# Layer 1 of a three-stage kernel: the next unit's square, tanh and cube ahead of this unit's cast and low part

## The chip, the cores and the metric

One core of one Trainium2 chip runs the whole program. The metric is the device time of one launch in microseconds (us), as the median of several runs. TensorE (PE) multiplies matrices into eight banks of PSUM; VectorE (DVE) and ScalarE (ACT) read those banks and do the elementwise work; the SyncE queue (SP) issues the DMA transfers. Each engine works through its own instructions in the order in which the program gives them.

## The reference, cut to what matters

```python
# 1. attention inside chunks of 64 tokens: q, k, v are (4, 8, 576, 64)
scores = scale * np.matmul(q_c, k_c.transpose(0, 1, 2, 4, 3))
scores = scores - np.max(scores, axis=-1, keepdims=True)
attn = np.exp(scores)
attn = attn / (np.sum(attn, axis=-1, keepdims=True) + 1e-09)
out = np.matmul(attn, v_c)
x = out ... reshaped to (2304, 512)
# 2. layer 1: w_in (512, 2048), w_out (2048, 512)
h = x @ w_in
x = (h - np.tanh(h)) @ w_out
# 3. layer 2: the same shapes, other weights
h = x @ w_in
sp = np.where(h > 20.0, h, np.log1p(np.exp(np.minimum(h, 20.0))))
out = (h * np.tanh(sp)) @ w_out
```

## The kernel before, in words

The 2304 tokens are 18 tiles of 128 (`i` = 0 to 17), gathered into five blocks of 512, 256, 512, 512 and 512 tokens; block 1 is the short one. The 2048 hidden features are 16 units of 128. One step `s` is one unit of one block of one layer, so there are 160 steps: layer 1 is steps 0 to 79 (block 0 is steps 0 to 15, the short block steps 16 to 31, block 4 steps 64 to 79), layer 2 is steps 80 to 159.

Every product is made of three matmuls on a split operand: a high part (the value rounded to the matmul's format) and a low part (what the rounding left). In step `s` PE runs `gemm1(s)` (12 matmuls into one "hidden" bank, 4 or 5 by turns in layer 1) and then `gemm2` of the unit two steps back (three back in the short block), 12 matmuls that add into banks 0 to 3. After a block's last `gemm2`, `evacuate` takes banks 0 to 3 out, with one cast on ACT and one subtraction on DVE for each bank.

Between the two products of layer 1 the value h - tanh(h) is made from six or seven instructions:

- `gap_act`: the square `z` (ACT L314) and the tanh `t` (ACT L315), both read from the hidden bank;
- `gap_mid`: the cube `g` = z * h (DVE L320) and h - t (DVE, helper line L69, tile `t`), both read from the hidden bank; the second is the bank's last reader;
- `gap_poly`: a mask `m` and a second square of `z` (ACT L325, L326), from SBUF;
- `gap_end`: the polynomial (DVE L307) and the choice between the two forms (DVE L308);
- `hi_part`: the cast to the high part `go` (ACT L334); `lo_part`: its low part (DVE L69, tile `go`).

`gap_end`, `hi_part` and `lo_part` of a unit stand one step later than the rest. In step `s` the order before is: `gemm1(s)`; for unit `s - 1` its `gap_end`, cast and low part; for unit `s` its square, tanh, cube, difference and polynomial; then `gemm2`.

While block 0 runs, the weights of layer 1 arrive as 64-bit words and are turned into high and low parts, one unit per step: `w_turned` (ACT L89), `w_low` (DVE L99), `w_float` (DVE L108), `w_hi` (ACT L117), `w_lo` (DVE L69, tile `w`). While block 4 of layer 1 runs, `convert2` does the same for layer 2 at one or two pieces per step.

The attention of block 0's four tiles is done ahead of step 0, in an order written out by hand (the lead, which `run(...)` lists). The attention of the other tiles is spread over the steps of the block before theirs, each tile starting three steps after the one ahead of it. The plan `inner` is run between the elementwise work and `gemm2`, the plan `tail` at the step's end. For a tile the steps are: `a_scores` (PE L180, into banks 6 and 7), `a_first` (the maximum L187 and its subtraction on DVE, the exp L192 on ACT), `a_norm` one step later (four DVE instructions L197 to L200), `a_turn` two steps later (four PE transposes L207), `a_turned` (ACT copy L212), and three steps later `a_values` (PE L224) and `a_parts` (a cast on ACT L236 and a low part on DVE). PE also runs `warm`, transposes of the identity whose result is not used.

All banks are one tensor, `banks`. The framework that orders the engines writes the waits from the program's order and from what each instruction touches.

Of the kernel before, what the change touches and what calls it, by code (L numbers as in the profile page):

```python
# [27 lines left out]
P = 128  # L28
# [4 lines left out]
NF = DFF // P  # L33
# [3 lines left out]
BLOCKS = [512, 256, 512, 512, 512]  # L37
TMAX = 512
# [3 lines left out]
def attn_moe_moe(ctx, tc, qkv, w1, w2, out):  # L42

    nc = tc.nc
# [3 lines left out]
    block_of = [max(b for b in range(NB) if first[b] <= i) for i in range(NI)]  # L48
# [10 lines left out]
    ident = const.tile([P, P], F32, name="ident")  # L59
# [3 lines left out]
    banks = psum.tile([P, 8, 512], F32, name="banks")  # L63
# [4 lines left out]
    def sub(o, a, b, eng=None):  # L68
        (eng or nc.vector).tensor_tensor(o, a, b, op=ALU.subtract)  # L69
# [26 lines left out]
    def w_low(layer, f):  # L96

        lo = w_words(layer, f, I32)[0]
        nc.vector.tensor_scalar(lo, lo, 29, None, op0=ALU.logical_shift_right)  # L99
# [14 lines left out]
    def w_hi(layer, f):  # L114
        del W[layer, f, "raw"]
        w = W[layer, f] = wp.tile([P, 2, 2 * DM], F32R, tag=f"w{f}", name=f"w{f}")
        nc.scalar.copy(w[:, 0], W[layer, f, "f"])  # L117

    def w_lo(layer, f):
        w = W[layer, f]  # L120
        sub(w[:, 1], W.pop((layer, f, "f")), w[:, 0].bitcast(F32))
# [23 lines left out]
    def cast2():  # L145
        while casts:
            w_hi(1, casts.pop(0))
# [13 lines left out]
    def pair(i, n):  # L161


        return banks[:, BK[i]:BK[i] + 2, n * 2 * P:(n + 1) * 2 * P]

    def room(i, tag, early):

        if i < first[1]:
            return ep.tile([P, TMAX], F32, tag=early[i // 2 % len(early)], name=tag)
        return pools["a"].tile([P, TMAX], F32, tag=tag, name=tag, bufs=1)  # L170
# [23 lines left out]
    def a_norm(i):  # L194
# [4 lines left out]
        nc.vector.reciprocal(rd, rd)  # L199
        nc.vector.tensor_tensor(e, e, rd[:].unsqueeze(3).to_broadcast([P, 2, NP, CH]), op=ALU.mult)  # L200

    def a_turn(i):

        e = E[i].rearrange("p j n k -> p (j n k)")
        ps = pair(i, 0)
        for n in range(NP):
            nc.tensor.transpose(ps[:, n // 2, n % 2 * P:(n % 2 + 1) * P], e[:, n * P:(n + 1) * P], ident)  # L207

    def a_turned(i):
        del E[i]  # L210
        ET[i] = room(i, "et", "t")[:].rearrange("p (n t) -> p n t", n=NP)
        nc.scalar.copy(ET[i].rearrange("p (m n) t -> p m n t", m=2),  # L212
                       pair(i, 0).rearrange("p m (n t) -> p m n t", n=2))

    def a_values(i):

# [28 lines left out]
    def hidden(s):  # L245
        l, b, f = steps[s]
        n = 4 + s % 2 if l == 0 else 4 + (s - HALF) % 4
        return banks[:, n, :BLOCKS[b]]

    def gemm1(s):  # L250
        l, b, f = steps[s]
        w, x, ps = W[l, f], XL[l, b], hidden(s)
        n = 0
        for k in range(KD):
            for a, c in ((0, 0), (0, 1), (1, 0)):
                nc.tensor.matmul(ps, w[:, a, k * P:(k + 1) * P], x[:, c, k, :BLOCKS[b]],  # L256
                                 start=n == 0, stop=n == 3 * KD - 1)
                n += 1
# [42 lines left out]
    def valid(s, l):  # L301
        return 0 <= s < NS and steps[s][0] == l


    def gap_end(s):
        z, t, m, g = ZT.pop(s)
        nc.vector.scalar_tensor_tensor(g, z, PK, g, op0=ALU.add, op1=ALU.mult)  # L307
        nc.vector.copy_predicated(g, m.bitcast(I16), t)  # L308
        GF[s] = g

    def gap_act(s):
        ph = hidden(s)
        z, t, m, g = ZT[s] = temp(s, "z"), temp(s, "t"), temp(s, "m", BF16), temp(s, "g")
        nc.scalar.activation(z, ph, AF.Square)  # L314
        nc.scalar.activation(t, ph, AF.Tanh)  # L315

    def gap_mid(s):
        ph = hidden(s)
        z, t, m, g = ZT[s]
        nc.vector.tensor_tensor(g, z, ph, op=ALU.mult)  # L320
        sub(t, ph, t)

    def gap_poly(s):
        z, t, m, g = ZT[s]
        nc.scalar.activation(m, z, AF.Relu, bias=-C2)  # L325
        nc.scalar.activation(z, z, AF.Square, scale=SQ_SCALE, bias=SQ_BIAS)  # L326

    def hi_part(s):
        if lag(s) > LAG and s % 2:

            o = GO[s] = op.tile([P, 2, TMAX], F32R, tag="o", name="go")
        else:
            o = GO[s] = gp.tile([P, 2, TMAX], F32R, tag="go", name="go")
        nc.scalar.copy(o[:, 0, :BLOCKS[steps[s][1]]], GF[s])  # L334

    def lo_part(s):
        t = BLOCKS[steps[s][1]]
        sub(GO[s][:, 1, :t], GF.pop(s), GO[s][:, 0, :t].bitcast(F32))

    def mish(s):  # L340
        g = GF[s] = temp(s, "g")
        nc.scalar.activation(g, hidden(s), AF.Mish)  # L342
# [10 lines left out]
    for f in range(NF - 2):  # L353
        w_load(0, f)

    def warm(n):

        for _ in range(n):
            nc.tensor.transpose(banks[:, 7, 2 * P:3 * P], ident, ident)

    def a_first(i):
        a_max(i)
# [2 lines left out]
    def a_turns(i):  # L365
        a_turn(i)
        a_turned(i)
# [5 lines left out]
    def run(*todo):  # L373
        for what, *args in todo:
            what(*args)


    warm(8)
    run((a_scores, 0), (a_scores, 1), (a_scores, 2), (a_first, 0), (a_first, 1), (a_norm, 0), (a_turns, 0),
        (a_first, 2), (a_norm, 1), (a_values, 0), (a_turns, 1), (a_scores, 3), (a_first, 3), (a_part, 0, 0),  # L380
        (a_norm, 2), (a_part, 0, 1), (a_values, 1), (a_turns, 2), (a_part, 1, 0), (w_turned, 0, 0),
        (a_norm, 3), (a_part, 1, 1), (w_low, 0, 0), (a_values, 2), (a_turns, 3), (a_part, 2, 0), (a_part, 2, 1),
        (w_float, 0, 0), (a_values, 3), (warm, 8), (w_hi, 0, 0), (a_part, 3, 0), (a_part, 3, 1), (w_lo, 0, 0),
        (w_turned, 0, 1), (w_low, 0, 1), (w_float, 0, 1),
        (a_load, lead), (a_load, lead + 1), (w_load, 0, NF - 2), (w_load, 0, NF - 1),
        (w_turned, 0, 2), (w_low, 0, 2))

# [2 lines left out]
    inner, tail = {}, {}  # L390

    def at(plan, s, *todo):
        plan.setdefault(s, []).extend(todo)

    for b in range(1, NB):
        for q in range(BLOCKS[b] // P):
            i = first[b] + q
            BK[i] = 6
            s = (b - 1) * NF + (2 if BLOCKS[b] > 2 * P else 5) + 3 * q
            at(inner, s, (a_scores, i))  # L400
            at(tail, s, (a_first, i))
            at(tail, s + 1, (a_norm, i))
            at(inner, s + 2, (a_turn, i))
            at(tail, s + 2, (a_turned, i))
            at(inner, s + 3, (a_values, i))
            at(tail, s + 3, (a_parts, i))
            if i + 2 < NI:
                at(tail, s + 3, (a_load, i + 2))

    LAG = 2  # L410
    done = 0
# [1 line left out]
    def lag(s):  # L413

        l, b, f = steps[s]
        return LAG + (l == 0 and BLOCKS[b] < TMAX)

    last = (NB - 1) * NF
    for s in range(NS + LAG):

        j = s - last
        if j == 0:
            es.close()
            pools["out"] = ctx.enter_context(tc.tile_pool(name="late", bufs=1))
        if s == HALF:
            nc.scalar.preload_act_table_set("mish")
        u = s + 2
        if s < NS:
            gemm1(s)
        if u - 1 < NF:  # L430
            w_hi(0, u - 1)
        if valid(s - 1, 0):
            gap_end(s - 1)
            hi_part(s - 1)
        if valid(s - 1, 1):
            hi_part(s - 1)
            lo_part(s - 1)
        if u - 1 < NF:
            w_lo(0, u - 1)
        if valid(s - 1, 0):  # L440
            lo_part(s - 1)
        if valid(s, 0):
            gap_act(s)
            gap_mid(s)
            gap_poly(s)
        if valid(s, 1):
            mish(s)
        cast2()
        run(*inner.get(s, []))
        if u < NF:  # L450
            w_float(0, u)
        while done < min(NS, s + 1) and done + lag(done) <= s:
            gemm2(done)
            done += 1
        if u + 1 < NF:
            w_turned(0, u + 1)
            w_low(0, u + 1)
        run(*tail.get(s, []))

        f = j - LAG - 1  # L460
        if 0 <= f < NF:
            w_load(1, f)
        f = j - LAG - 3
        if 0 <= f < NF:
            (w_turned if f < TURNED else w_rebias)(1, f)
        if LAG + 5 <= j < NF:
            convert2(1 if j % 3 else 2, j - LAG - 4)
        elif j >= NF and j != NF + 1:
            convert2(2, j - LAG - 4)
        if s < NS:  # L470
            l, b, f = steps[s]
            if f == 5 and l == 0 and b == NB - 1:
                x_load(0)
            if f == 5 and l == 1 and b + 1 < NB:
                x_load(b + 1)
# [37 lines left out]
```

## Time and profile before

| | |
|---|---|
| median of 3 runs | 890.13 us (890.1 to 890.99) |
| the profiled execution's own time | 888.45 us |
| its span, first to last instruction | 886.7 us |
| busy: PE, DVE, ACT | 843.2, 480.8, 400.6 us |
| mean granted clock of TensorE | 0.988 |

The profiled execution took 1.75 us more than its span, and 1.68 us less than the median of the runs. Busy times are sums over instructions; a busy PE is not PE at its peak, since the ends of matmuls are modelled.

### The profile page before, as it was taken

Reading aid. Unit: us, or ns where it says so; the run is one execution under the profiler, and the core shown is the slowest. Engines: PE = TensorE matmul, PEld = TensorE weight load, DVE = VectorE, ACT = ScalarE, POOL = GpSimd, SP = SyncE. Lnnn points to the kernel's source line nnn. Section 1 sums busy time; section 2 is a strip of 40 time slices with the busy share of each in tenths; the row PEclk is TensorE's granted clock in tenths of the full one; section 3 lists DMA queues with packets and bytes.
Section 4 is the critical chain, followed back from the end, with each engine's and each line's share of the span. In section 5 each row is a group of like instructions: output and inputs, shape, how many; then the busy total and the mean of one; then the engine's idle time right before and its main releaser. Section 6 shows DMA issues by size and latency. Waiting matters only on the chain.

```text
span 886.7 us, 12059 instructions
## 1 busy us (share of the span) xinstructions
PE 843.2 (95%) x4984; PEld 700.0 (79%) x4984; DVE 480.8 (54%) x736; ACT 400.6 (45%) x704; POOL 6.4 (1%) x11
## 2 busy tenths in 40 slices
PE   5798898989999999999998999999999999999998
PEld 4586777887888878888886788898888888888886
DVE  5799997776777677767788984111111111111111
ACT  3677775555555555455776543232222222222221
POOL 0000000000000000000001000000000000000000
PEclk9799999999999999999999999999999999999999
DMA  9940102221111131006754510030300030001001
GB/s 375 420 178 6 60 7 96 72 70 51 37 37 36 59 109 36 1 1 214 295 199 147 183 55 1 1 143 1 119 0 1 1 143 0 1 1 48 0 1 48
DMA packets 16903, 72.08 MB, mean 81 GB/s; under 512 B 1488, under 2 KB 3536, under 8 KB 12240
## 3 DMA queue, kind: packets, MB, share of 16 engines
q1 hardware_dynamic: 16848, 71.31, 21.7%
q8 instruction: 39, 0.64, 0.3%
q14 instruction: 16, 0.13, 0.1%
HBM read 57.15 MB, written 14.16 MB: 80 GB/s over the span
## 4 chain that ended last, share of the span: by engine, by line
PE 69%; DVE 21%; ACT 6%; issue 1%; ACTq 0%
PE banks L256 33%; PE banks L270 22%; PE banks L267 12%; DVE g L320 3%; DVE wf L108 3%; DVE g L308 3%; DVE g L307 2%; DVE w L69 2%; DVE t L69 2%; ACT go L334 2%; ACT z L314 2%; ACT t L315 2%; DVE w L99 1%; DVE x L69 1%; DVE go L69 1%; ACT z L326 1%
## 5 line engine op out<-in xcount | busy, mean ns | idle before, releaser
L256 PE MATMUL banks<-x,w 128*128 128x512 f32 (+1 forms) x1920 | 426.2, 371 | 7.6 <-ACT w L117 3.1
L256 PEld LDWEIGHTS banks<-x,w 128*128 128x128 f32 x1920 | 340.0, 190 | 73.2 <-DVE w L69 5.2
L69 DVE TENSOR_TENSOR go<-g,go 128x512 fp32r<-128x512 f32 (+1 forms) x160 | 102.4, 640 | 321.2 <-ACT go L334 321.1
L267 PE MATMUL banks<-go,w 128*128 128x512 f32 (+1 forms) x960 | 217.4, 375 | 6.1 <-ACT go L334 3.5
L270 PE MATMUL banks<-w,go 128*128 128x512 f32 x864 | 209.0, 389 | 0.0
L334 ACT CAST go<-g 128x512 fp32r<-128x512 f32 (+1 forms) x160 | 92.5, 578 | 252.3 <-PE banks L270 136.3
L267 PEld LDWEIGHTS banks<-go,w 128*128 128x128 f32 x960 | 167.7, 190 | 39.2 <-ACT go L334 4.8
L270 PEld LDWEIGHTS banks<-w,go 128*128 128x128 f32 x864 | 161.2, 188 | 32.8 <-DVE x L69 0.2
L342 ACT ACTIVATE g<-banks 128x512 f32<-128x512 f32 (+1 forms) x80 | 44.5, 556 | 140.0 <-PE banks L256 139.2
L320 DVE TENSOR_TENSOR g<-z,banks 128x512 f32<-128x512 f32 (+1 forms) x80 | 50.7, 634 | 28.8 <-ACT t L315 26.7
L326 ACT ACTIVATE z<-z 128x512 f32<-128x512 f32 (+1 forms) x80 | 47.2, 590 | 23.9 <-DVE g L320 23.9
L308 DVE COPY_PREDICATED g<-m,t 128x512 f32<-128x512 int16 (+1 forms) x80 | 54.7, 684 | 2.8
L307 DVE SCALAR_TENSOR_TENSOR g<-z,g 128x512 f32<-128x512 f32 (+1 forms) x80 | 50.6, 633 | 5.2 <-ACT z L326 5.2
L69 DVE TENSOR_TENSOR t<-banks,t 128x512 f32<-128x512 f32 (+1 forms) x80 | 50.4, 630 | 0.0
L314 ACT ACTIVATE z<-banks 128x512 f32<-128x512 f32 (+1 forms) x80 | 44.1, 551 | 10.3 <-PE banks L256 10.2
L325 ACT ACTIVATE m<-z 128x512 bf16<-128x512 f32 (+1 forms) x80 | 47.0, 588 | 0.0
L315 ACT ACTIVATE t<-banks 128x512 f32<-128x512 f32 (+1 forms) x80 | 43.8, 548 | 0.0
L69 DVE TENSOR_TENSOR w<-wf,w 128x1024 fp32r<-128x1024 f32 x32 | 39.1, 1223 | 2.8 <-ACT w L117 2.8
L117 ACT CAST w<-wf 128x1024 fp32r<-128x1024 f32 x32 | 33.5, 1046 | 5.0 <-DVE wf L108 5.0
L207 PE MATMUL banks<-ident,e 128*128 128x128 f32 x72 | 13.2, 313 | 19.2 <-DVE e L200 19.2
L69 DVE TENSOR_TENSOR x<-banks,x 128x512 fp32r<-128x512 f32 (+1 forms) x38 | 23.8, 659 | 14.1 <-ACT x L236 10.7
L192 ACT ACTIVATE e<-e 128x512 f32<-128x512 f32 x18 | 11.4, 632 | 36.1 <-DVE e L69 36.1
(33 smaller groups left out, 274.0 us busy)
## 6 DMA issues: line engine op xcount, KB each, us to landing
w<-w SPq DMA_DIRECT2D x32, 1024.0 KB, 10.4
qkv<-qkv SPq DMA_DIRECT2D x18, 768.0 KB, 4.5
x<-x SPq DMA_DIRECT2D x16, 512.0 KB, 4.3
x<-x SPq DMA_DIRECT2D x4, 2048.0 KB, 8.5
out<-out SPq DMA_DIRECT2D x18, 256.0 KB, 2.1
x<-x SPq DMA_DIRECT2D x4, 256.0 KB, 2.7
x<-x SPq DMA_DIRECT2D x1, 1024.0 KB, 8.5
```

Of the source, the lines that this page charges most:

```text
L69: (eng or nc.vector).tensor_tensor(o, a, b, op=ALU.subtract)
L256: nc.tensor.matmul(ps, w[:, a, k * P:(k + 1) * P], x[:, c, k, :BLOCKS[b]], start=n == 0, stop=n == 3 * KD - 1)
L267: nc.tensor.matmul(banks[:, m, :t], w[:, a, DM + m * P:DM + (m + 1) * P], g[:, c, :t], start=start, stop=stop)
L270: nc.tensor.matmul(banks[:, m], g[:, a, m * P:(m + 1) * P], w[:, c, DM:], start=start, stop=stop)
L307: nc.vector.scalar_tensor_tensor(g, z, PK, g, op0=ALU.add, op1=ALU.mult)
L308: nc.vector.copy_predicated(g, m.bitcast(I16), t)
L314: nc.scalar.activation(z, ph, AF.Square)
L315: nc.scalar.activation(t, ph, AF.Tanh)
L320: nc.vector.tensor_tensor(g, z, ph, op=ALU.mult)
L325: nc.scalar.activation(m, z, AF.Relu, bias=-C2)
L326: nc.scalar.activation(z, z, AF.Square, scale=SQ_SCALE, bias=SQ_BIAS)
L334: nc.scalar.copy(o[:, 0, :BLOCKS[steps[s][1]]], GF[s])
```

## The change

In layer 1 the step's order becomes: `gemm1(s)`; `gap_end(s - 1)`; `w_lo` of the next weights; square, tanh, cube and difference of unit `s`; the cast of unit `s - 1`; mask and second square of unit `s`; the low part of unit `s - 1`. For the four tiles of block 2 (6 to 9), whose attention runs under the short block, scores, maximum, exp and norm come one step earlier, transposes and values stay in the step where they were, and the transposes are written to the second half of banks 4 and 5 (`turn_room`) where the short block's `gemm1` fills only the first half. The lead is written in another order, with more `warm` transposes, and those in bank 5 in place of 7, save for the last eight.

```diff
+    def short(i):
+        return block_of[i] > 0 and BLOCKS[block_of[i] - 1] < TMAX
...
+    def turn_room(i):
+        if short(i):
+
+            return banks[:, 4:6, 2 * P:4 * P]
+        return pair(i, 0)
+
     def a_turn(i):
-        ps = pair(i, 0)
+        ps = turn_room(i)
...
         nc.scalar.copy(ET[i].rearrange("p (m n) t -> p m n t", m=2),
-                       pair(i, 0).rearrange("p m (n t) -> p m n t", n=2))
+                       turn_room(i).rearrange("p m (n t) -> p m n t", n=2))
...
-    def warm(n):
+    def warm(n, bank=7):
         for _ in range(n):
-            nc.tensor.transpose(banks[:, 7, 2 * P:3 * P], ident, ident)
+            nc.tensor.transpose(banks[:, bank, 2 * P:3 * P], ident, ident)
...
-    warm(8)
-    run((a_scores, 0), (a_scores, 1), (a_scores, 2), (a_first, 0), (a_first, 1), (a_norm, 0), (a_turns, 0),
-        (a_first, 2), (a_norm, 1), (a_values, 0), (a_turns, 1), (a_scores, 3), (a_first, 3), (a_part, 0, 0),
-        (a_norm, 2), (a_part, 0, 1), (a_values, 1), (a_turns, 2), (a_part, 1, 0), (w_turned, 0, 0),
-        (a_norm, 3), (a_part, 1, 1), (w_low, 0, 0), (a_values, 2), (a_turns, 3), (a_part, 2, 0), (a_part, 2, 1),
-        (w_float, 0, 0), (a_values, 3), (warm, 8), (w_hi, 0, 0), (a_part, 3, 0), (a_part, 3, 1), (w_lo, 0, 0),
-        (w_turned, 0, 1), (w_low, 0, 1), (w_float, 0, 1),
+    run((warm, 14, 5), (a_scores, 0), (warm, 2, 5), (a_scores, 1), (warm, 2, 5), (a_scores, 2), (warm, 4, 5),
+        (a_first, 0), (a_first, 1), (a_norm, 0), (a_turn, 0), (a_scores, 3), (a_turned, 0), (a_first, 2),
+        (a_norm, 1), (a_values, 0), (a_turn, 1), (w_turned, 0, 0), (a_max, 3), (a_part, 0, 0), (a_turned, 1),
+        (a_exp, 3), (a_norm, 2), (a_values, 1), (a_turn, 2), (a_part, 0, 1), (a_part, 1, 0), (a_turned, 2),
+        (a_norm, 3), (a_values, 2), (a_turn, 3), (a_part, 1, 1), (w_low, 0, 0), (w_float, 0, 0), (a_part, 2, 0),
+        (a_turned, 3), (a_part, 2, 1), (a_values, 3), (warm, 8), (w_hi, 0, 0), (w_low, 0, 1), (a_part, 3, 0),
+        (w_lo, 0, 0), (a_part, 3, 1), (w_turned, 0, 1), (w_float, 0, 1),
         (a_load, lead), (a_load, lead + 1), (w_load, 0, NF - 2), (w_load, 0, NF - 1),
         (w_turned, 0, 2), (w_low, 0, 2))
...
-            s = (b - 1) * NF + (2 if BLOCKS[b] > 2 * P else 5) + 3 * q
+            s = (b - 1) * NF + (1 if short(i) else 2 if BLOCKS[b] > 2 * P else 5) + 3 * q
             at(inner, s, (a_scores, i))
             at(tail, s, (a_first, i))
             at(tail, s + 1, (a_norm, i))
-            at(inner, s + 2, (a_turn, i))
-            at(tail, s + 2, (a_turned, i))
-            at(inner, s + 3, (a_values, i))
-            at(tail, s + 3, (a_parts, i))
+
+            t = s + 2 + short(i)
+            at(inner, t, (a_turn, i))
+            at(tail, t, (a_turned, i))
+            at(inner, t + 1, (a_values, i))
+            at(tail, t + 1, (a_parts, i))
             if i + 2 < NI:
-                at(tail, s + 3, (a_load, i + 2))
+                at(tail, t + 1, (a_load, i + 2))
...
         if valid(s - 1, 0):
             gap_end(s - 1)
-            hi_part(s - 1)
...
         if u - 1 < NF:
             w_lo(0, u - 1)
-        if valid(s - 1, 0):
-            lo_part(s - 1)
         if valid(s, 0):
             gap_act(s)
             gap_mid(s)
+        if valid(s - 1, 0):
+            hi_part(s - 1)
+        if valid(s, 0):
             gap_poly(s)
+        if valid(s - 1, 0):
+            lo_part(s - 1)
```

## Rows read from the trace of the kernel before

**Rows 1.** The page's busy time of each engine, with its share of the span.

```profile
PE 843.2 (95%) x4984; PEld 700.0 (79%) x4984; DVE 480.8 (54%) x736; ACT 400.6 (45%) x704; POOL 6.4 (1%) x11
```

**Rows 2.** Windows: stretch, its length, busy us and instructions by engine, granted clock, DMA.

```profile
0.00:28.97 28.97, 16.37 (x288) 13.07 (x288) 16.43 (x31) 10.86 (x16) 0.70 (x6) 0.88 0.95 385
47.66:133.04 85.38, 78.14 (x449) 61.90 (x448) 82.76 (x114) 62.18 (x95) 0.00 (x0) 0.98 0.13 49
218.19:492.00 273.81, 269.51 (x1630) 219.25 (x1628) 204.92 (x310) 161.37 (x278) 3.40 (x3) 1.00 0.27 97
```

**Rows 3.** Waits of PE, 133 to 200 us: us in total, times, longest.

```profile
PE banks L207 <- DVE e L200: 9.6, 4, 4.0
```

**Rows 4.** Waits of PE, 470 to 495 us.

```profile
PE banks L267 <- ACT go L334: 3.5, 3, 1.4
```

**Rows 5.** Timeline of the lead and step 0: start, us, instruction, idle before it.

```profile
1.36 1.97 PE L359 MATMUL banks<-ident 128*128 128x128 f32 x8 [1.36 <-POOL ident masks.py:199]
...
16.75 0.69 DVE L187 TENSOR_REDUCE mx<-banks 128x8 f32<-128x512 f32 x1 [2.30 <-PE banks L180]
...
28.23 0.69 DVE L69 TENSOR_TENSOR x<-banks,x 128x512 fp32r<-128x512 f32 x1 [1.65 <-ACT x L236]
...
30.11 6.88 PE L256 MATMUL banks<-x,w 128*128 128x512 f32 x22 [0.40 <-DVE w L69]
...
35.38 0.69 DVE L320 TENSOR_TENSOR g<-z,banks 128x512 f32<-128x512 f32 x1 [1.05 <-ACT t L315]
```

**Rows 6.** Timeline of SP's queue: the weight loads issued first.

```profile
2.96 24.58 SPq L75 DMA_DIRECT2D w<-w  x14
```

**Rows 7.** DMA issues of 2.9 to 3.2 us: transfers, KB each, us to landing.

```profile
w<-w SPq DMA_DIRECT2D x1, 1024.0 KB, 11.8
```

**Rows 8.** A window of 2 us within step 0's first product.

```profile
32.00:34.00 2.00, 2.00 (x6) 1.54 (x5) 1.49 (x2) 1.04 (x1) 0.00 (x0) 0.50 1.02 426
```

**Rows 9.** Timeline of one step of block 0.

```profile
52.93 0.68 DVE L69 TENSOR_TENSOR go<-g,go 128x512 fp32r<-128x512 f32 x1
53.02 0.59 ACT L315 ACTIVATE t<-banks 128x512 f32<-128x512 f32 x1
...
53.64 0.69 DVE L320 TENSOR_TENSOR g<-z,banks 128x512 f32<-128x512 f32 x1
54.24 0.68 DVE L69 TENSOR_TENSOR t<-banks,t 128x512 f32<-128x512 f32 x1
```

**Rows 10.** The cube's line over the whole trace: idle before it, us and times.

```profile
  ACT t L315: 26.7, 51
```

**Rows 11.** Windows from one tile's transposes to the next's in the short block.

```profile
152.58:166.20 13.62, 12.06 (x140) 11.66 (x140) 9.61 (x23) 6.73 (x18) 0.00 (x0) 0.87 0.17 59
166.20:178.78 12.58, 10.56 (x140) 10.16 (x140) 9.63 (x23) 6.64 (x18) 0.00 (x0) 1.00 0.20 64
```

**Rows 12.** Timeline of the short block around one tile's transposes.

```profile
178.78 0.66 PE L207 MATMUL banks<-ident,e 128*128 128x128 f32 x4 [2.02 <-DVE e L200]
...
179.90 0.38 ACT L314 ACTIVATE z<-banks 128x256 f32<-128x256 f32 x1
...
180.03 0.42 DVE L69 TENSOR_TENSOR go<-g,go 128x256 fp32r<-128x256 f32 x1 [0.47 <-ACT go L334]
...
180.93 0.42 DVE L69 TENSOR_TENSOR t<-banks,t 128x256 f32<-128x256 f32 x1
...
182.75 0.65 PE L180 MATMUL banks<-qkv 64*64 64x64 f32 x32
```

**Rows 13.** Timeline: PE at the end of the short block's evacuation.

```profile
215.34 3.02 PE L267 MATMUL banks<-go,w 128*128 128x512 f32 x12 [1.98 <-DVE x L69]
```

**Rows 14.** Timeline of one step of block 4, layer 2's weights in conversion.

```profile
471.03 0.69 DVE L69 TENSOR_TENSOR go<-g,go 128x512 fp32r<-128x512 f32 x1 [0.74 <-ACT go L334]
...
472.01 0.69 DVE L320 TENSOR_TENSOR g<-z,banks 128x512 f32<-128x512 f32 x1 [0.29 <-ACT t L315]
```

**Rows 15.** Chain of waits that ended last, a full-clock stretch: start, us, what.

```profile
236.49 2.72 PE banks L256 x12
```

## Prediction

> **What bounds the kernel now.** I read the page's busy times first: PE is busy for 95% of the span, 843.2 us, so 43.5 us of idle PE is about all that an order of instructions can win, apart from slow clock [rows 1]. Then the windows by stage, which show where the idle time lies. In the lead (0 to 29 us) PE is busy 16.4 of 29.0 us; in block 0, DVE is busy 82.8 of 85.4 us and PE 78.1, so DVE sets the pace; from 218 to 492 us PE is busy 269.5 of 273.8 us, so the 512-token blocks of layer 1 are bound by PE but for 4.3 us [rows 2]. Next the waits of PE. In the short block, PE waits four times at a tile's transposes for that tile's norm, 9.6 us in all [rows 3]; late in block 4 it waits for the cast and the low part of the unit that `gemm2` needs, 3.5 us for the cast alone, which is most of the 4.3 [rows 2, 4]. Last the timelines of these places, for what each engine waits for in turn. The gain is thus to be sought in four places: lead, block 0, short block, end of block 4.
>
> **The lead.** DVE waits there three times that the new order touches: 2.30 us for the scores of tile 3, which stood behind tile 1's transposes, 1.65 us for the cast of tile 3 [rows 5], and about 1 us more between. With scores 3 right behind tile 0's transposes, DVE goes from tile 1's norm straight to tile 3's maximum, 2.4 us earlier. I followed the new list with the durations that the trace has for the same instructions: tile 3's low part, on which the first `gemm1` waits, ends near 25.2 to 26.0 us in place of 28.92 [rows 5]. A new wait: `w_turned` of unit 0 is moved up in ACT's queue to about 13.6 us, and its weights land at 2.96 + 11.8 = 14.8 us [rows 6, 7]. Behind it wait tile 0's cast, tile 1's copy and tile 3's exp; this costs ACT 1.2 us but tile 3's norm on DVE, their first consumer on the path, still finds the exp done, so I take 0.3 us at the end.
>
> The first `gemm1` then runs 12 matmuls. Of the 22 that began at 30.11, ten finished the first `gemm1` by about 34.2 us, for the square was free to start at 35.38 - 1.05 - 0.1 [rows 5]: about 0.41 us each, at a granted clock of 0.50 (1.2 GHz) [rows 8]. At full clock 12 take 2.72 us [rows 15]; at half clock 4.95. So it ends between 25.2 + 2.7 = 27.9 and 26.0 + 4.95 = 31.0, and the first cube comes 1.14 us later, at 29.1 to 32.1 in place of 35.38: a gain of 3.3 to 6.3 us. The new lead leaves PE shorter pauses, so I take 5.0, a little above the middle. The cost of the extra `warm` transposes is nothing while they fit into the wait for q and k; they do at 14 x 0.25 us from 1.36 us on [rows 5], and the later groups of two and four also end before the next arrival. If they didn't, each would cost at most 0.25 us.
>
> **Block 0.** Here DVE works without pause, so only what shortens its own sequence counts. The cube starts at 53.64, when ACT's tanh has ended (53.02 + 0.59), and 0.71 us after the low part started; independent instructions follow each other at 0.60 (53.64 to 54.24) [rows 9]. With square and tanh ahead of the cast, the tanh is done before DVE comes to the cube, which saves 0.11 us in some eleven steps, 1.2 us. One step gives 0.3 back, where PE, just past a wait for a norm, delivers its hidden bank late. Net 0.9. Cast and low part are later by about 1.2 us; `gemm2` needs them only a step later.
>
> **The short block.** The same reordering cuts DVE's wait for the cast (0.47 us a step here [rows 12]), but PE decides. The four waits for a norm go, since now a step lies between norm and transposes. What is late next is the place that the transposes write: banks 4 and 5, where ACT and DVE still read this step's hidden bank. Do instructions that touch different columns of a bank wait for each other? The cube needs only `z` and the bank, yet it starts when the tanh, a mere reader of the same bank, has ended; 26.7 us of idle time in 51 places end so [rows 10]. No row shows it for different columns, so the bounds are: no wait, or a wait until the bank's last reader, the difference, is done. I take the wait, being the nearest row. From the square's start to the difference's end are 180.93 + 0.42 - 179.90 = 1.45 us [rows 12]; with 0.05 to start, PE stands 1.5 us in place of 2.02 [rows 12]. A period of three steps is PE's 10.56 us of work plus that: 12.1 in place of 12.58 [rows 11]. DVE agrees: its 9.63 us of work [rows 11] plus a wait for the scores (0.8) and one for the next square and tanh (1.4) is 11.8. Three periods: gain 1.4.
>
> The Trainium skill's page "PSUM — Partial Sum Buffer", section "PSUM bank collisions raise a hardware error", says that two engines at one bank collide also at disjoint columns and that waits should guard the bank and not the address. By it the transposes wait and the sum is the one below; by the rows alone, which show one range of columns, the time of rival (a) stays open too. The trace agrees as far as the cube's waits go [rows 10]; no row shows other columns.
>
> Against this stand two losses at the block's start. Scores of tile 6 move ahead of the last `gemm2` of block 0, 0.6 us of PE [rows 12]. And DVE, on which the first transposes wait in either order, does one unit more between the evacuation and them: choice, polynomial, cube and difference, four instructions of 0.42, 1.7 us, against two waits of 0.47 for a cast that it no longer has [rows 12]: 0.7 later. The drop of the clock to 0.87 in the first period [rows 11] follows a 4.0 us wait [rows 3], and there is one as long now. 1.4 - 0.6 - 0.7 - 0.4 for the clock (the scores now run in it too) = -0.3.
>
> At the block's end the evacuation stands behind ACT's square of `z`; with square and tanh before the cast that comes 0.7 us earlier, and PE's wait of 1.98 us [rows 13] shrinks as much: +0.7.
>
> **Block 4.** With layer 2's weights in conversion DVE falls behind, by the low part's wait for its cast, 0.74, and the cube's for the tanh, 0.29, a step [rows 14]. Both go: the cube and the difference now lie between the choice and the low part while the cast runs. That is 1.03 us a step over nine steps against the 4.3 us that PE idles [rows 2], after which PE's 2 x 2.72 = 5.44 us a step [rows 15] binds again. I take 4.0.
>
> **Elsewhere** blocks 2 to 4 stay bound by PE: a cast now waits for its step's `gemm1` and the low part ends some 3 us behind it, while `gemm2` needs it 5.4 us behind it. The loads of q, k and v keep their step and are issued as before. Layer 2 is untouched.
>
> **Sum.** 5.0 + 0.9 - 0.3 + 0.7 + 4.0 = 10.3 us. The profiled execution's 888.45 becomes 878.15 (span 886.7 to 876.4); the median of the runs shown lies 1.68 us above it, so 879.8.
>
> **Rivals.** (a) Transposes in another half of a bank don't wait. Then the four waits of 9.6 us [rows 3] go, and the slow clock of the first period with them (1.0, 13.62 against 12.58 [rows 11]), less the 0.6 + 0.7 lost at the start: 9.3 in place of -0.3, 870.2. For it speaks that DVE's 9.63 is less than PE's 10.56; against it the cube's waits. 0.17. (b) The lead stays at half clock, and ACT's wait for the weights reaches the path: 3.0 in place of 5.0 there, and with the cold start of the short block worse by 2, a sum of 6.3: 883.8. For it speaks the clock of 0.50 at 32 us [rows 8], against it the shorter pauses. 0.15. (c) Slower: the later cast binds in the PE-bound steps. It decides once the low part ends more than 5.4 us behind `gemm1`; at 0.5 us beyond, in some 45 steps of blocks 2 to 4, it costs 22 us against 10.3: 891.6. Against it speak 2.4 us of slack and PE's 269.5 of 273.8 [rows 2]; a tile's maximum and norm take up to 2 us of DVE but stand behind the low part. 0.03. (d) Nothing moves, since what the lead wins is waited for later: the DMA or a wait that I don't see. 889 to 891. 0.03.
>
> **Numbers.** The forecast has 0.62, with its own range 876 to 883. The whole range must leave out 2 in 10: 868 to 885 takes in (a) and most of (b). Changes under 0.2% (1.8 us) can't be told from none. Faster: 0.62 + 0.17 + 0.15 = 0.94; same 0.03; slower 0.03.
>
> **What would show it.** The first square near 29 to 31 us; in block 0 cube pitches of 0.60 behind the weights' low part; at the short block's transposes waits of PE for the difference (tile `t`) in place of the norm; no wait for `go` at 470 to 495 us; DVE idle before a low part near none. Wrong would be: transposes that start right behind `gemm1`, a first `gemm1` past 27 us, or waits of `gemm2` for `go` in blocks 2 and 3.

## The result and the profile after

The changed kernel takes **879.23 us** (median of 4, 877.69 to 882.58) against 890.12 us before in the same measurement: ratio **0.9884 [0.9853, 0.9915]**, so 10.3 us faster by the ratio, at the least 7.6 (the medians lie 10.9 apart). Predicted were 879.8 us and 10.3 us.

The profiled execution of the changed kernel, 882.58 us with a span of 880.8, is the longest of its four; the same kernel measured again (`e1_after_again` below) took 878.77, and its profiled execution 879.07 with a span of 877.3. Both traces are used, since they differ where the clock does.

The page's busy times after:

```profile
PE 848.1 (96%) x4998; PEld 706.7 (80%) x4998; DVE 471.8 (54%) x736; ACT 400.1 (45%) x704; POOL 6.9 (1%) x11
```

Against [rows 1], PE has 14 instructions more (the added `warm` transposes) and 32.7 us idle in place of 43.5. DVE's busy time fell by 9 us with the same 736 instructions, whose durations add up to 502.8 us before and 503.7 after. So the page's busy time is not the sum over instructions that it was called above: two that follow each other without a wait start 0.60 us apart and last 0.69 [rows 9], the time in which they overlap counts once, and more of them now overlap.

Where the time went is read by cutting both spans at the same instructions: the first `gemm1`, the first `gemm1` of the short block (step 16) and of block 2 (step 32), that of step 35, which follows the evacuation's wait, and the first `gemm2` of layer 2. Windows of before (columns: stretch, length, busy us and instructions of PE, PEld, DVE, ACT, POOL, granted clock, DMA share, GB/s):

```profile
29.00:133.04 104.04, 93.19 (x496) 73.06 (x497) 99.69 (x135) 75.56 (x114) 0.00 (x0) 0.95 0.29 115
133.04:199.85 66.81, 57.02 (x645) 54.02 (x644) 50.23 (x112) 35.84 (x97) 0.00 (x0) 0.97 0.23 79
199.85:218.19 18.34, 16.36 (x118) 13.86 (x117) 13.53 (x25) 10.69 (x23) 0.00 (x0) 1.00 0.10 34
218.19:497.52 279.33, 274.90 (x1653) 223.58 (x1652) 209.41 (x315) 165.59 (x285) 3.40 (x3) 1.00 0.27 95
```

The same of the changed kernel, the profiled execution of the result:

```profile
24.79:129.16 104.37, 94.14 (x497) 74.69 (x497) 97.70 (x135) 75.67 (x114) 0.00 (x0) 0.93 0.33 131
129.16:200.98 71.82, 62.40 (x645) 58.36 (x644) 47.80 (x112) 36.17 (x96) 0.00 (x0) 0.90 0.22 74
200.98:218.70 17.72, 16.36 (x118) 13.85 (x117) 12.78 (x24) 10.14 (x22) 0.00 (x0) 1.00 0.10 34
218.70:491.59 272.89, 272.89 (x1654) 224.06 (x1652) 204.37 (x315) 164.37 (x284) 3.36 (x3) 1.00 0.27 97
```

And of the same kernel measured again, with its periods of three steps in the short block, from one tile's transposes to the next's, behind them:

```profile
25.32:127.80 102.48, 90.89 (x498) 71.27 (x497) 97.75 (x135) 76.09 (x115) 0.00 (x0) 0.98 0.33 132
127.80:197.62 69.82, 60.42 (x645) 56.43 (x644) 47.78 (x112) 36.22 (x96) 0.00 (x0) 0.93 0.22 77
197.62:215.34 17.72, 16.36 (x118) 13.86 (x117) 12.76 (x24) 10.14 (x22) 0.00 (x0) 1.00 0.10 34
215.34:488.20 272.86, 272.86 (x1654) 224.30 (x1653) 204.20 (x316) 165.35 (x286) 3.80 (x3) 1.00 0.27 97
...
147.56:162.59 15.03, 13.45 (x142) 12.56 (x143) 9.21 (x23) 6.87 (x19) 0.00 (x0) 0.82 0.17 54
162.59:175.10 12.51, 10.70 (x139) 10.07 (x139) 9.22 (x23) 6.84 (x19) 0.00 (x0) 1.00 0.19 64
175.10:189.33 14.23, 12.63 (x142) 11.96 (x142) 9.21 (x23) 6.86 (x19) 0.00 (x0) 0.88 0.17 56
```

| gain in us, span of before 886.7 | predicted | result's execution | measured again |
|---|---|---|---|
| up to the first `gemm1` of the short block (lead and block 0) | 5.9 | 3.88 | 5.24 |
| short block | -0.3 | -5.01 | -3.01 |
| steps 32 to 35, with the evacuation | 0.7 | 0.62 | 0.62 |
| rest of blocks 2 to 4 | 4.0 | 6.44 | 6.47 |
| rest (layer 2 and end) | 0 | -0.03 | 0.08 |
| sum | 10.3 | 5.9 | 9.4 |

The first line is 133.04 less 129.16 and 127.80; the others are the differences of the lengths above, the last that of what follows 497.52, 491.59 and 488.20 up to the span's end. In the trace measured again the sum comes near because two misses cancel: the short block lost 2.7 us more than predicted, and block 4 gave 2.5 more.

The lead of the changed kernel, whole timeline (start, us, engine, line, instruction, idle before it):

```profile
13.07 1.13 ACT L89 ACTIVATE wf<-w 128x1024 f32<-128x1024 f32 x1
13.79 0.68 DVE L191 TENSOR_REDUCE mx<-banks 128x8 f32<-128x512 f32 x1
...
24.79 7.75 PE L266 MATMUL banks<-x,w 128*128 128x512 f32 x24 [0.53 <-DVE x L69]
...
30.98 0.69 DVE L330 TENSOR_TENSOR g<-z,banks 128x512 f32<-128x512 f32 x1 [2.76 <-ACT t L325]
```

Against [rows 5], DVE comes to tile 3's maximum at 13.79 in place of 16.75 without a wait, the first `gemm1` starts at 24.79, and the first cube at 30.98 in place of 35.38 (30.11 when measured again).

The waits of PE between 130 and 200 us (total us, times, longest), against [rows 3]:

```profile
PE banks L217 <- DVE t L69: 9.0, 4, 4.0
```

The waits for the norm are gone, and four waits for the difference (tile `t`) of nearly the same length stand in their place. The timeline of the short block shows how (the same columns):

```profile
148.45 0.42 DVE L69 TENSOR_TENSOR t<-banks,t 128x256 f32<-128x256 f32 x1
...
148.93 1.12 PE L217 MATMUL banks<-ident,e 128*128 128x128 f32 x4 [4.00 <-DVE t L69]
...
151.04 2.93 PE L277 MATMUL banks<-go,w 128*128 128x256 f32 x12
...
162.51 0.38 PE L217 MATMUL banks<-ident,e 128*128 128x128 f32 x2
...
164.02 0.42 DVE L69 TENSOR_TENSOR t<-banks,t 128x256 f32<-128x256 f32 x1
...
164.49 0.44 PE L217 MATMUL banks<-ident,e 128*128 128x128 f32 x2 [1.60 <-DVE t L69]
```

The transposes write the second half of banks 4 and 5; the difference that they wait for reads the hidden product in the first half of one of them. At 162.51 the two into bank 4 start right behind `gemm1`; the two into bank 5 start at 164.49, 0.05 us after the difference ends (164.02 + 0.42). So the wait is by bank. It is a wait that stands in the program; whether the chip would need it no run here shows. The price is not only the wait: behind the first, 12 matmuls of 256 columns took 2.93 us, at a granted clock of 0.50 (1.2 GHz, 151.04 to 153.76 us), where 1.70 is usual at 1.00 (2.4 GHz).

Block 4, timeline of the changed kernel with layer 2's weights in conversion, against [rows 14]:

```profile
477.01 0.68 DVE L330 TENSOR_TENSOR g<-z,banks 128x512 f32<-128x512 f32 x1
477.60 0.69 DVE L69 TENSOR_TENSOR t<-banks,t 128x512 f32<-128x512 f32 x1
...
478.20 1.37 DVE L69 TENSOR_TENSOR go<-g,go 128x512 fp32r<-128x512 f32 x1
```

Cube, difference and low part follow each other without a wait. (The low part's 1.37 us, twice its usual 0.69, falls together with POOL's work on the next weights, L94, 477.91 to 479.03; that is not looked into here.) PE has none of the waits of [rows 4] left: from 214 to 470 us it waits once, 1.36 us at the evacuation (1.98 in [rows 13]), and from 470 to 495 never. DVE's idle time before the cube grew from the 26.7 us of [rows 10] to 85.6 us in 54 places; that is DVE waiting in steps that PE sets, for a `gemm1` that isn't done, and costs nothing.

### The profile page after: what moved, and what is told of

Read it like the earlier page. It is cut to its first block, busy times and chain, and to the rows that moved or that the text cites. A ratio compares the mean times of both kernels' runs of the same rounds, so it can differ in the third digit from the quotient of the medians.

```text
span 880.8 us, 12081 instructions
## 1 busy us (share of the span) xinstructions
PE 848.1 (96%) x4998; PEld 706.7 (80%) x4998; DVE 471.8 (54%) x736; ACT 400.1 (45%) x704; POOL 6.9 (1%) x11
## 4 chain that ended last, share of the span: by engine, by line
PE 86%; DVE 9%; ACT 2%; issue 1%; DMA 1%; SPq 0%; ACTq 0%
PE banks L266 41%; PE banks L280 22%; PE banks L277 20%; DVE wf L108 1%; PE banks L217 1%; DVE x L69 1%; DVE g L330 1%; PE banks L184 1%; DVE e L204 1%; PE banks L234 1%; DVE t L69 1%; DVE g L318 1%; DVE g L317 1%; DVE w L99 1%; DVE rd L201 1%
## 5 line engine op out<-in xcount | busy, mean ns | idle before, releaser
L277 PE MATMUL banks<-go,w 128*128 128x512 f32 (+1 forms) x960 | 220.5, 380 | 1.4 <-DVE x L69 1.4
L277 PEld LDWEIGHTS banks<-go,w 128*128 128x128 f32 x960 | 171.7, 196 | 32.9 <-DVE x L69 1.6
L330 DVE TENSOR_TENSOR g<-z,banks 128x512 f32<-128x512 f32 (+1 forms) x80 | 50.6, 632 | 85.7 <-ACT t L325 85.6
```

Of the source, the lines that this page charges most:

```text
L277: nc.tensor.matmul(banks[:, m, :t], w[:, a, DM + m * P:DM + (m + 1) * P], g[:, c, :t], start=start, stop=stop)
```

## The experiments

**Theory A**, the prediction's mechanism with its price corrected: the short block's transposes wait for the last reader of banks 4 and 5 although the columns differ, and each such wait is paid a second time in slow clock behind it; the other parts bring what the table says. **Theory B**, the rival: the columns decide and the bank doesn't, so the loss in the short block belongs to that one execution or to DVE's own work, and other banks would bring nothing. Each expectation says in numbers what to see in its run. All kernels compute the whole reference. "Stretch" is the short block from its first `gemm1` to the first behind it: 66.81 us before.

**`e1_after_again`: the changed kernel once more.** No edit.

> The changed kernel once more, unchanged, as the yardstick for the others on this chip. Theory A (transposes in banks 4 and 5 wait for the hidden bank's last reader): 878 to 881 us, PE waits at the transposes near 9 us, all for the difference (tile t), and from the short block's fifth gemm1 to the first of block 2 some 55 to 58 us. Theory B (the waits at the transposes are not what holds the short block; the slow clock of the one profiled execution is): the same stretch comes back near 48 us in another execution, with the same waits.

878.77 us against 890.21 before, 0.9866 [0.9852, 0.9881]. The waits for `t` were again 9.0 us in four places, the stretch 69.82 us; from the fifth `gemm1` on, as the expectation counts, 55.75. The waits are a property of the program; what differs between executions is the clock behind them: after the wait of 1.58 us at 162.59 the next 12 matmuls took 1.70 us here (granted clock 1.00), after the 1.60 us at 164.49 in the result's execution 2.77 (0.54). The period behind that wait, to be read against the one of 12.51 us above:

```profile
164.49:178.49 14.00, 12.18 (x138) 11.54 (x138) 9.21 (x23) 6.83 (x19) 0.00 (x0) 0.88 0.18 57
```

So "each such wait is paid a second time" is too strong: of the four waits, three were followed by slow matmuls (2.77 to 2.93 us) in the result's execution and two (2.93 and 2.55) here; behind the last wait 12 took 1.68 in both.

**`e2_free_turns`: the transposes to another bank.** The short block's transposes go to the second half of banks 6 and 7.

```
 def turn_room(i):
     if short(i):
-        return banks[:, 4:6, 2 * P:4 * P]
+        return pair(i, 1)
```

> The changed kernel, with the short block's transposes written to the second half of banks 6 and 7 in place of 4 and 5; all steps stay as they are. Theory A: no reader of the hidden bank stands in the way, the wait for the difference goes (9 us to under 2), the clock stays up, a period of three steps falls from about 14 to 10.6 to 11.5 us, and the run to 866 to 871 us. Theory B (DVE's own work of 9.6 us a period with its waits sets the pace, wherever the transposes are written): PE waits move to another line, the time stays within 2 us of the changed kernel.

868.56 us, 0.976 [0.9741, 0.9778]: 9.4 us faster than the changed kernel (0.9866 - 0.976). PE timeline and windows, from one tile's transposes to the next's:

```profile
156.16 0.60 PE L217 MATMUL banks<-ident,e 128*128 128x128 f32 x4
...
156.16:167.50 11.34, 10.78 (x143) 10.31 (x141) 9.21 (x24) 6.65 (x19) 0.00 (x0) 1.00 0.21 71
167.50:178.83 11.33, 10.77 (x142) 10.30 (x141) 9.20 (x24) 6.63 (x19) 0.00 (x0) 1.00 0.20 71
```

All four transposes run together, and no wait for the difference is left; only the first tile's still wait, 0.40 us for its norm. The period is 11.3 us at a granted clock of 1.00 (the first, 12.67, has a wait of the values), and the stretch 59.95. Theory A holds as to the wait, B falls: same step, same order, same kind of half bank, only the bank differs. The Trainium skill, page "PSUM — Partial Sum Buffer", section "PSUM bank collisions raise a hardware error", asks to guard a bank whichever columns are used; the waits of 9.0 us with shared banks and none with others agree that this program is guarded so.

**`e3_order_only`: before with the order of the step alone** (the last hunk of the change).

> The kernel before, with only the order within a step changed (square, tanh, cube and difference ahead of the cast and the low part). Theory A: the 6 us that PE gained at the end of block 4 come from this alone, block 0 gains under 1 us because PE there binds next, the old transposes keep their waits for the norm (9 to 10 us): 882 to 884.5 us. Theory B (the end of block 4 gained because the lead put PE and DVE elsewhere relative to each other): 887 us or more, with waits of gemm2 for go left at the end of block 4.

878.55 us, 0.9868 [0.9854, 0.9883]: as much as the whole change. The stretch fell by 3.2 us to 63.62, though the transposes are where they were; waits of PE, 130 to 200 us:

```profile
PE banks L207 <- DVE e L200: 6.9, 4, 2.7
```

So the order alone shortens DVE's way to the norm (9.6 us in [rows 3]). Blocks 2 to 4 won 6.5 us (from step 35 to layer 2 272.82 us against 279.33 before), the evacuation 0.6, and up to step 16 nothing (133.50 against 133.04). The time lies below the ranges of both theories: A named the places, but took too little for the short block and for block 4.

**`e4_short_only`: before with the short block's part alone.**

```
+    def short(i): ...
-            s = ... + (2 if BLOCKS[b] > 2 * P else 5) + 3 * q
+            s = ... + (1 if short(i) else 2 if BLOCKS[b] > 2 * P else 5) + 3 * q
+            t = s + 2 + short(i)
```

> The kernel before, with only the short block's attention changed (scores, maximum and norm a step earlier, transposes into the second half of banks 4 and 5). Theory A: the wait for the norm is replaced by one for the difference of the same size or longer, since DVE still waits for the cast in front of it: 890 to 893 us, not faster than before. Theory B: the norm's wait goes without a successor, 882 to 885 us.

908.48 us, 1.0208 [1.0191, 1.0225]: 18.5 us slower, where a few had been expected. Waits of PE, 130 to 220 us, and one row of its timeline:

```profile
PE banks L217 <- DVE t L69: 15.5, 6, 5.6
...
230.88 4.39 PE L277 MATMUL banks<-go,w 128*128 128x512 f32 x11 [1.98 <-DVE x L69]
```

The same waits by bank, 15.5 us, since in the old order each difference also stands behind the low part and its wait of 0.47 us for the cast [rows 12]. The slow clock behind them comes on top (stretch 81.72). At the evacuation a wait of 1.98 us, the very length of [rows 13], was followed by 11 matmuls in 4.39 us (the view ends there; all 12 took 4.62, at a granted clock of 0.62), where 12 took 3.02 at 1.00 there.

**`e5_lead_only`: before with the new lead alone.**

> The kernel before, with only the lead in its new order and with its added warm transposes. Theory A (the lead's 5 us go through block 0, which DVE paces, to the end): 884.5 to 886 us. Theory B (what the lead wins is waited for later): the first cube comes 4 to 5 us earlier, the first gemm1 of the short block less than 2 us earlier, 888 us or more.

886.08 against 890.89, 0.9944 [0.9926, 0.9963]: 5.0 us. The first `gemm1` starts at 25.24, the first cube at 30.49. The first `gemm1` of the short block comes at 128.80 in place of 133.04, so most of what the lead wins goes through block 0 (Theory A). In this execution `w_turned` did wait for its weights (it starts at 14.70, after 1.46 us for the DMA), and yet the first `gemm1` lies between the two of the changed kernel (24.79 and 25.32).

**`e6_no_short`: the change without the short block's part.**

```
 def short(i):
-    return block_of[i] > 0 and BLOCKS[block_of[i] - 1] < TMAX
+    return False
```

> The changed kernel without its short-block part: new lead, new order within a step, but scores, norm and transposes of the short block in their old steps and old banks. Theory A (the three parts add up, and the short block's part costs 5 us): 872.5 to 875 us, so faster than the whole change. Theory B (the earlier scores pay once the order is new): 878 us or more.

873.08, 0.9801 [0.9786, 0.9817]. That is Theory A's range: the short block's part costs the changed kernel 5.8 us (0.9866 - 0.9801), the intervals being apart. Stretch 63.61, as with the order alone.

**`e7_fill_wait`: idle transposes in the wait.** Ten transposes of the identity into bank 7 ahead of each of the short block's transposes, so that PE works while it would stand.

```
+            if short(i):
+                at(inner, t, (warm, 10))
             at(inner, t, (a_turn, i))
```

> The changed kernel, with ten transposes of the identity into bank 7 put ahead of the short block's transposes of each tile, where PE waits anyway. Theory A (beyond the wait itself, the slow clock that follows it costs 2 to 4 us): the granted clock of the periods rises from 0.82 to 0.88 towards 1.00, each takes 12.5 us in place of 14 to 15, and the run 874.5 to 877 us. Theory B (the wait for the difference alone is the cost): the periods stay over 13.5 us or the clock changes nothing, 878.5 us or more.

874.56, 0.9832 [0.9802, 0.9861], with a stretch of 66.02. PE timeline:

```profile
156.84 1.25 PE L369 MATMUL banks<-ident 128*128 128x128 f32 x10
157.93 0.38 PE L217 MATMUL banks<-ident,e 128*128 128x128 f32 x2
158.81 0.44 PE L217 MATMUL banks<-ident,e 128*128 128x128 f32 x2 [0.50 <-DVE t L69]
159.81 1.70 PE L277 MATMUL banks<-go,w 128*128 128x256 f32 x12
```

More work on the same path, and 3.8 us less of stretch: `gemm2` behind the wait takes 1.70 us. The transposes still wait for the difference; what is gone is the slow clock behind the wait (granted clock 1.00 over the whole stretch, where `e1_after_again` has 0.93). This holds for the traced execution. One of the four, 879.29 us at a mean clock of 0.981, was as long as the changed kernel, and the intervals of the two overlap a little, so the transposes are not shown to keep the clock up every time.

**`e9_values_late`: `e2_free_turns` with the values behind `gemm2`.**

```
-            at(inner, t + 1, (a_values, i))
+            at(tail if short(i) else inner, t + 1, (a_values, i))
```

> The kernel with the transposes in banks 6 and 7 (868.6 us), with the short block's values product moved behind gemm2 of its step, so that it no longer waits in front of gemm2 for the next tile's maximum, which reads the same two banks (3.0 us in three waits). Theory A: these waits go and 865.5 to 867.5 us follow. Theory B (PE is paced by DVE there anyway): the wait returns at another line, 868 to 870 us.

867.08, 0.9741 [0.9723, 0.9759], stretch 58.67. PE's waits at the values between 44 and 480 us fall from 3.0 us to 1.2:

```profile
PE banks L234 <- DVE e L69: 1.2, 3, 0.4
```

The wait is again by bank: the values write the second half of banks 6 and 7, the next tile's maximum reads the first. By the times the kernel isn't told apart from `e2_free_turns`.

**`e10_block0_too`: the same for the tiles whose attention runs under block 0** (scores to norm a step earlier, transposes to the other half of banks 6 and 7), on top of `e9_values_late`.

```
-    return block_of[i] > 0 and BLOCKS[block_of[i] - 1] < TMAX
+    return block_of[i] in (1, 2)
...
-            s = (b - 1) * NF + (1 if short(i) else 2 if BLOCKS[b] > 2 * P else 5) + 3 * q
+            s = (b - 1) * NF + (4 if b == 1 else 1 if short(i) else 2) + 3 * q
```

> The kernel with the late values (867.1 us), with tiles 4 and 5, whose attention runs in block 0, treated in the same way: scores, maximum and norm a step earlier, transposes in banks 6 and 7 in their old step. PE waits 5.5 us for their norms before. Theory A (PE and DVE now both bind in block 0): part of the wait comes back, 864.5 to 866.5 us. Theory B (DVE alone paces block 0): the wait goes, the first gemm1 of the short block does not come earlier, 866.5 to 868 us; slower if the tile's q, k and v have not landed a step earlier.

866.73 against 890.1, 0.9736 [0.9723, 0.9749]: no gain that can be told from `e9_values_late`. Waits of PE, 44 to 480 us, first of `e9_values_late`, then of this kernel:

```profile
PE banks L217 <- DVE e L204: 5.8, 3, 2.7
```

```profile
PE banks L266 <- DVE w L69: 5.5, 4, 2.6
...
PE banks L217 <- DVE e L204: 0.4, 1, 0.4
```

The wait for the norm goes, and as much appears at `gemm1`, for the weights' low part: DVE is behind in block 0, and PE waits for it at one place or another. The first `gemm1` of the short block comes no earlier (127.12 against 126.23), as Theory B has it. These last two are the fastest kernels found, 2.6% faster than before.

**`e8_few_warm`: the new lead without its extra `warm` transposes.**

```
-    run((warm, 14, 5), (a_scores, 0), (warm, 2, 5), (a_scores, 1), (warm, 2, 5), (a_scores, 2), (warm, 4, 5),
+    run((warm, 8, 5), (a_scores, 0), (a_scores, 1), (a_scores, 2),
```

> The changed kernel with eight warm transposes at the lead's start and none between the scores, so the lead's order without its added warm transposes. Theory A (the order of scores and norms makes the lead's gain, the added transposes only speed PE's pieces, which DVE covers): the first cube comes at 30 to 31.5 us, the run takes 878 to 880.5 us. Theory B (the clock that the added transposes raise makes the gain): scores, transposes and values in the lead at half clock throughout, the first gemm1 near 5 us long, the first cube at 32 us or later, 880.5 to 883 us.

880.31 (six executions, 877.73 to 882.91), 0.9883 [0.9861, 0.9905]: not told apart from the changed kernel, whose eight executions of both measurements go from 877.42 to 882.58. The six fall into two groups, three below 878.1 and three above 882.5, and the traced one is of the second. What the extra transposes do stays open; the new order of the lead keeps its gain without them (first cube at 31.29).

**`e11_low_only`: half of the new order.** Before, with the low part moved behind cube and difference, but the cast left ahead of square and tanh.

```
 gap_end(s - 1); hi_part(s - 1); ...
-if valid(s - 1, 0):
-    lo_part(s - 1)
 gap_act(s); gap_mid(s); gap_poly(s)
+if valid(s - 1, 0):
+    lo_part(s - 1)
```

> The kernel before, with half of the new order: the low part stands behind the cube and the difference, but the cast stays ahead of the square and the tanh on ACT. Theory A (both the cast's and the low part's place matter): DVE no longer waits for the cast, but the cube now waits for cast, square and tanh in a row, 1.75 us behind the choice, more than the 0.74 and 0.29 before; the waits for go at the end of block 4 grow, 890 to 897 us. Theory B (the low part's place is what counts): 878 to 884 us.

915.16, 1.027 [1.0247, 1.0294]: 24 us slower, as to its sign expected, as to its size not. Up to the short block it is 7.7 us longer than before, in the short block 7.4, from step 35 to layer 2 11.8. Its timeline in block 0, and DVE's waits there (36 to 140 us):

```profile
89.62 0.74 DVE L308 COPY_PREDICATED g<-m,t 128x512 f32<-128x512 int16 x1
...
90.25 1.21 DVE L69 TENSOR_TENSOR w<-wf,w 128x1024 fp32r<-128x1024 f32 x1
90.45 0.62 ACT L334 CAST go<-g 128x512 fp32r<-128x512 f32 x1 [0.98 <-DVE g L308]
...
90.98 0.59 ACT L314 ACTIVATE z<-banks 128x512 f32<-128x512 f32 x1
...
91.47 0.59 ACT L315 ACTIVATE t<-banks 128x512 f32<-128x512 f32 x1
...
92.09 0.69 DVE L320 TENSOR_TENSOR g<-z,banks 128x512 f32<-128x512 f32 x1 [0.62 <-ACT t L315]
...
DVE g L320 <- ACT t L315: 9.5, 15, 1.6
```

After the choice (L308) ACT does the cast, then the square, then the tanh, and the cube needs the tanh. In the kernel before, the low part of `go` filled that time on DVE; moved behind the cube, it leaves DVE idle for 0.62 us a step, 9.5 us in 15 steps of block 0, where DVE sets the pace. With the cast moved behind the tanh as well, square and tanh no longer wait for the choice, and the hole is closed. The low part's move thus needs the cast's; the cast's move alone was not run.

**How the parts add.** By the ratios of the runs: lead -5.0 us, order -11.8, short block's part +18.5, in sum +1.7; together they give -11.9 (0.9866). The short block's part costs 18.5 with the old order and 5.8 with the new one.

## Why the prediction was right

The places and the waits were named rightly in the main. That the sum comes within 1 us is in part luck: the short block and block 4 were each missed by about 2.5 us, in opposite directions.

**The lead (5.0): right.** The first cube came 4.40 and 5.27 us earlier in the two executions, 4.89 with the lead alone (`e5_lead_only`). Start of `gemm1` and cube lie in or, by 0.4 us, ahead of the ranges given. The feared wait for the weights came in one execution and not in the other.

**Block 0 (0.9): right on DVE, nothing on PE.** Step 14's cube starts at 128.45 before and 121.85 in the second trace of the changed kernel, 6.60 us earlier, of which 5.27 came from the lead: DVE won 1.3 (0.84 in the result's execution, 5.24 less 4.40). But the short block's first `gemm1` comes only 5.24 earlier; in both executions the way from that cube to this `gemm1` grew by 1.36 us. With the order alone (`e3_order_only`, 133.50 against 133.04) the `gemm1` comes no earlier at all. By the end of block 0 PE sets the pace (full timeline, changed kernel measured again):

```profile
121.85 0.68 DVE L330 TENSOR_TENSOR g<-z,banks 128x512 f32<-128x512 f32 x1
122.36 2.88 PE L266 MATMUL banks<-x,w 128*128 128x512 f32 x12
...
126.40 0.69 DVE L330 TENSOR_TENSOR g<-z,banks 128x512 f32<-128x512 f32 x1 [1.29 <-ACT t L325]
```

DVE waits 1.29 us for a tanh whose `gemm1` has only just ended. The step that failed is "DVE sets the pace": it was true of the stage's mean, not of its last steps.

**The short block (-0.3): right mechanism, mis-sized.** The question that the prediction left to the nearest row, whether other columns of a bank wait, was answered as taken, bank by bank: for two of the four tiles the two transposes into the other bank did start right behind `gemm1`, the prediction's sign of being wrong, and the other two waited. Rival (a) fell by the 9.0 us of waits, and `e2_free_turns` shows what it would have given (868.56; rival (a) said 870.2). The term came out at -3.01. By its pieces, from the second trace: three periods of 12.1 and 1.44 us of slow clock (1.04 as before, 0.4 more) make 37.7; measured were three times 12.51 with 4.24 us of slow clock in the first and third (15.03 - 12.51 and 14.23 - 12.51), 41.8. So 1.2 us of the miss is the period and **2.8 us the clock, the piece most mis-sized**: I priced the clock once, for the first period, where it cost 2.52 and not 1.44, and it fell again behind a later wait, for 1.72. `e7_fill_wait` shows it from the other side, in its traced execution. Against that, the 1.3 us of losses at the block's start came to 0.22 (19.76 us from step 16 to the first transposes against 19.54), and the block's end gave 0.2. Nor did the prediction see that the order alone, with the transposes left in place, gains 3.2 us here; the move of the transposes spent that and 3 more.

**The evacuation (0.7): right**, 0.62, as the wait went from 1.98 to 1.36.

**Block 4 (4.0): right mechanism, too small.** 6.4 us. The term was capped by PE's idle time of 4.3 us, but the windows of before show 274.90 us of busy PE in that stretch, and after 272.89 for one matmul more: 2.0 us of standing had been counted as busy, since ends of matmuls are modelled. The pitch shows a part of it, in one of three such places. PE's timeline of before:

```profile
471.05 0.50 PE L267 MATMUL banks<-go,w 128*128 128x512 f32 x1 [1.16 <-ACT go L334]
471.77 2.79 PE L267 MATMUL banks<-go,w 128*128 128x512 f32 x11 [0.23 <-DVE go L69]
```

One matmul fills 0.72 us to the next, where [rows 15] give 0.23 each: PE stood for 0.49, of which only 0.23 are listed.

**Elsewhere and rivals.** No wait of PE for `go` appears in blocks 2 to 4, so (c) didn't come. (Its time was added up wrongly: 22 us on top of 879.8 is 901.8, not 891.6.) `e11_low_only` shows a reordering of the same instructions that is slower, though in the stages that DVE paces more than by a late `gemm2`. That nothing moves, (d), fell with the first result. (b) is half seen: in the result's execution the first product did run at a granted clock of 0.50 (1.2 GHz) and its short block was 2 us worse, and its time was 882.58, near (b)'s 883.8, but ACT's wait for the weights, (b)'s other half, was not in it; in the other trace the clock was 0.84 in the same window, and 879.07 came out. Windows of two us within the first product, first of the result's execution, then of the kernel measured again:

```profile
26.00:28.00 2.00, 2.00 (x7) 1.52 (x6) 1.50 (x2) 0.95 (x1) 0.00 (x0) 0.50 1.03 430
```

```profile
26.00:28.00 2.00, 2.00 (x9) 1.64 (x8) 1.48 (x3) 1.47 (x2) 0.00 (x0) 0.84 1.05 438
```

## What to carry to other kernels

Before results are put into the free half of a bank, ask who reads the other half and when: by the choice of bank alone, the same move of a step cost 5.8 us or gained some 3.6 (`e2_free_turns` against `e6_no_short`, 0.976 and 0.9801). For every wait of PE, price the slow clock that can follow it too; and read what removing it can win from the pitch of the matmuls, not from listed idle time. Undo each part of a change by itself: this one is 1.2% faster, and 2.0% without one of its three parts.

## What the runs showed of the hardware

The same wait does not always cost the clock. 1.98 us at the evacuation was followed by 12 matmuls in 3.02 us in [rows 13] (granted clock 1.00, 2.4 GHz), but in 4.61 us in `e5_lead_only` and 4.62 in `e4_short_only` (0.62 in both, a mean of the two levels); behind a wait of 1.6 us in the short block 12 matmuls took 1.70 us in one execution (1.00) and 2.77 in another of the same kernel (0.54). What decides between them was not tried. With ten transposes of the identity within the wait, the traced execution of `e7_fill_wait` has 1.68 to 1.70 us behind all four, at a granted clock of 1.00, with waits of 0.49 to 2.90 us left.
